# A new fixed TensorE order for an interleaved recurrent-attention and GLU kernel

## The chip, the cores and the metric

The kernel runs on one core of one Trainium2 chip. The metric is the device time of one execution in microseconds (us). The engines are named as the profile names them: PE is TensorE's matmul side, PEld its weight load, DVE is VectorE, ACT is ScalarE, POOL is GpSimd, and SP is SyncE, which here issues almost all DMAs. All of them run from their own instruction stream and meet only at semaphores.

## What is computed

A memory-augmented attention block and a gated GLU block alternate, four blocks in all, over a sequence of 2048 rows of width 448. Cut to what matters:

```
def A(x):                       # 16 heads of 256, segments of 32 rows, 8 memory rows
    mem = mem0
    for s in range(64):
        h = concat(mem, x[32*s : 32*s+32])            # 40 rows
        q, k, v = h @ Wq, h @ Wk, h @ Wv              # per head
        p = softmax(mask(q @ k.T / 16))
        o = sum over heads of (p @ v) @ Wo
        mem, out[s] = o[:8], o[8:]                    # the next segment needs this mem
def B(x):
    g = x @ W_gate
    return ((g * (g > 0)) * (x @ W_up)) @ W_down
x = x + A(layernorm(x));  x = x + B(layernorm(x))     # layer 0
x = x + A(layernorm(x));  x = x + B(layernorm(x))     # layer 1, same weights
```

The memory makes A a recurrence of 64 segments: segment s+1 cannot start its scores before `mem` of segment s is there.

## The kernel before, in words

**Set-up.** The weights of a head are folded: `M` (from Wq and Wk) gives the scores directly from h, `N` (from Wv and Wo) gives the output directly from p @ h. These products are made once, while the weights arrive by DMA.

**Steps.** After that come 68 steps (`step`, L1382). In step t, segment t of layer 0 and segment t-4 of layer 1 are worked on together, so nearly every operation handles 2 x 40 rows. Steps 0 to 3 have layer 0 alone, steps 64 to 67 layer 1 alone. A step has these PE groups, each one a run of matmuls that ends with one semaphore increment:

- `t_block` (L980): M times h; three blocks named 0, 1 and 2, each with a first part "f" on 64-row tiles and the rest "r" on the full array. ACT and DVE copy the result to `TTm` (memory rows) and `TTs` (segment rows).
- `s_mem` (L1054), the scores of the memory rows; then a softmax on DVE and ACT that ends in `Pm`; `p_t_mem` (L1127), a transpose of it on PE; a copy to `PTm`; `u_mem` (L1144), p @ h; a copy to `UTm` by ACT and DVE, half each; `un_mem` (L1158), times N; ACT copies a half to `sumA`, DVE adds the halves to `mv`, the new memory (L1176); `m_t` (L1178) transposes it for the next step. This is the recurrence.
- `s_seg` (L1076), the scores of the segment rows; a softmax on DVE and ACT that ends in `Ps`; a transposing DMA to `PTs` (`seg_pt`, L1117); four groups `u_seg0` to `u_seg3` (L1231); copies to `U` or `UTm`.
- Every second step: `un` (L1274), 28 pairs or quadruples of matmuls, U times N; a layernorm (`ln_b`, L944); a transposing DMA to `xBT`; `b_layer` (L1312), gate and up products in units of 4, 4, 4 and 2 column chunks; relu on ACT and a product on DVE to `hB`; `b_down`, seven groups. `un` and B work of one step is spread over the following steps, where it fills PE while the recurrence waits.

`m_nat` (L1201) moves the new memory with four small DMAs ("mk") and two more ("ride").

**What sets the order.** A planner inside the program (`_Order`, L320 to L510) places all 8371 operations on the engines, with a cost model of its own, before anything is emitted. Each operation has a key, and among those that could go next the smallest key wins. Keys of PE groups come from the table `SLOT` (L174), which names a group, its number and its step: `@a0` to `@a3` for the first four steps, `@z0` to `@z5` from step 64 on, and `@0` to `@3` for the step modulo 4 in between; `PERIOD` (L173) is added for every four steps. Keys of other engines' operations follow from who needs them, plus an offset from `BIAS` (L164). For steps 8 to 63 the order of the PE groups is not left to the planner: sorted by key they are chained, each a predecessor of the next (L375). So in this steady part the numbers in `SLOT` matter only by their rank, and the same order repeats every four steps. For the first and last steps they are priorities. The PSUM bank of a group, and whether a copy goes to ACT or DVE (`cp` allows both), are decided by the planner in both parts.

```
            if o.slot in SLOT:
                o.key = SLOT[o.slot] + PERIOD * (o.t // 4)
...
            o.key += sum(BIAS.get(k, 0.0) for k in bias_keys(o))
            o.prio = -o.key
        line = sorted((o for o in self.ops if o.slot in SLOT and 2 * LAG <= o.t < NSEG), key=lambda o: o.key)
        for a, b in zip(line, line[1:]):
            if a not in b.preds:
                b.preds.append(a)
```

A PE group has a mode, the tiling of the array it uses (0 whole array; 2 four column strips of 32; 3 quarters of 64 x 64). `un` and full `b_down` groups may run in mode 0 or, split into four column strips (`quarters`, L884), in mode 2; they take the mode that the array is in (L465). PSUM has eight banks, and a group that opens a new tile waits until the copies that read the bank before are done.

Of the kernel before, what the change touches and what calls it, by code (L numbers as in the profile page):

```python
# [45 lines left out]
class _Sched:  # L46
# [118 lines left out]
    "t_blockm+": 4131, "t_blocks+": 6194, "s_mem+": -350, "p_t_mem+": 7632, "u_mem+": -471, "un_mem+": -457,  # L165
    "un_memh+": -23541, "m_t+": -19808, "m_tk+": -8621, "s_seg+": -19261, "seg_pt+": -2390, "u_seg0+": -23506,
    "u_seg1+": 9252, "u_seg2+": -29593, "u_seg3+": -6650, "m_nat+": 10625, "t_block0f+": 14052, "t_block0r+": -1099,
    "t_block1r+": 22222, "t_block2r+": -17971, "ln_a+": 2217, "ln_ac+": 3345, "un+": -2521, "ln_b+": 1019,
    "b_layer+": -20861, "b_down+": -10132, "m_natx+": 7129, "stay": 2496, "win": 163,
# [5 lines left out]
    "t_block0f.0@a0": 50159, "t_block0r.0@a0": 48445, "t_block0r.1@a0": 66618, "t_block0r.2@a0": 58400,  # L175
    "t_block0r.3@a0": 37177, "t_block0r.4@a0": 67166, "t_block0r.5@a0": 95580, "t_block1f.0@a0": 81552,
    "t_block1r.0@a0": 96466, "t_block1r.1@a0": 76789, "t_block1r.2@a0": 77518, "t_block1r.3@a0": 84652,
    "t_block2r.0@a0": 4656, "s_mem.0@a0": 55973, "fills_mem.0@a0": 52862, "fills_mem.1@a0": 79245,
    "p_t_mem.0@a0": 77938, "u_mem.0@a0": -1119, "fillu_mem.0@a0": 107569, "un_mem.0@a0": 80345, "m_t.0@a0": 42261,
    "s_seg.0@a0": 71567, "u_seg0.0@a0": 100936, "u_seg1.0@a0": 91440, "u_seg2.0@a0": 80408, "u_seg3.0@a0": 56794,  # L180
    "t_block0f.0@a1": 45270, "t_block0r.0@a1": 17400, "t_block0r.1@a1": -7010, "t_block0r.2@a1": 40391,
    "t_block0r.3@a1": 82450, "t_block0r.4@a1": 52995, "t_block0r.5@a1": 62740, "t_block1f.0@a1": 63553,
    "t_block1r.0@a1": 28364, "t_block1r.1@a1": 74689, "t_block1r.2@a1": 76929, "t_block1r.3@a1": 81822,
    "t_block2r.0@a1": 67618, "s_mem.0@a1": 27449, "fills_mem.0@a1": 71144, "fills_mem.1@a1": 63924,
    "p_t_mem.0@a1": 6422, "u_mem.0@a1": 74228, "fillu_mem.0@a1": 51559, "un_mem.0@a1": 53034, "m_t.0@a1": 68700,
    "s_seg.0@a1": 67452, "u_seg0.0@a1": 69786, "u_seg1.0@a1": 83046, "u_seg2.0@a1": 92206, "u_seg3.0@a1": 76576,
    "un0.0@a1": 92765, "un0.1@a1": 79387, "un0.2@a1": 101487, "un0.3@a1": 90435, "un1.0@a1": 63322, "un1.1@a1": 69781,
    "un1.2@a1": 39275, "un1.3@a1": 40361, "un2.0@a1": 106250, "un2.1@a1": 82903, "un2.2@a1": 63137, "un2.3@a1": 42476,
    "un3.0@a1": 64407, "un3.1@a1": 71224, "b_layerf.0@a1": 139224, "b_layer.0@a1": 116387, "b_layer.1@a1": 98718,
    "b_layerf.1@a1": 143708, "b_layer.2@a1": 132409, "b_layer.3@a1": 103128, "b_down.0@a1": 127683,  # L190
    "b_down.1@a1": 126220, "b_down.2@a1": 72769, "b_down.3@a1": 112103, "b_down.4@a1": 96440, "b_down.5@a1": 113434,
    "b_down.6@a1": 125266, "t_block0f.0@a2": 37971, "t_block0r.0@a2": 12506, "t_block0r.1@a2": 60559,
    "t_block0r.2@a2": 46755, "t_block0r.3@a2": 83848, "t_block0r.4@a2": 58924, "t_block0r.5@a2": 46186,
    "t_block1f.0@a2": 28635, "t_block1r.0@a2": 60990, "t_block1r.1@a2": 72547, "t_block1r.2@a2": 53785,
    "t_block1r.3@a2": 60218, "t_block2r.0@a2": 66386, "s_mem.0@a2": 81137, "p_t_mem.0@a2": 78840, "u_mem.0@a2": 59588,
    "un_mem.0@a2": 43030, "m_t.0@a2": 39632, "s_seg.0@a2": 79148, "u_seg0.0@a2": 120824, "u_seg1.0@a2": 115627,
    "u_seg2.0@a2": 122511, "u_seg3.0@a2": 108587, "t_block0f.0@a3": 110070, "t_block0r.0@a3": 140639,
    "t_block0r.1@a3": 112726, "t_block0r.2@a3": 82684, "t_block0r.3@a3": 118188, "t_block0r.4@a3": 132793,
    "t_block0r.5@a3": 95384, "t_block1f.0@a3": 76944, "t_block1r.0@a3": 139308, "t_block1r.1@a3": 124186,
    "t_block1r.2@a3": 80065, "t_block1r.3@a3": 112387, "t_block2r.0@a3": 115734, "s_mem.0@a3": 142810,  # L200
    "p_t_mem.0@a3": 106030, "u_mem.0@a3": 151505, "un_mem.0@a3": 101197, "m_t.0@a3": 76094, "s_seg.0@a3": 97187,
    "u_seg0.0@a3": 127310, "u_seg1.0@a3": 89485, "u_seg2.0@a3": 145237, "u_seg3.0@a3": 114347, "un0.0@a3": 135091,
    "un0.1@a3": 98232, "un0.2@a3": 102557, "un0.3@a3": 118395, "un1.0@a3": 118579, "un1.1@a3": 58610,
    "un1.2@a3": 62740, "un1.3@a3": 81468, "un2.0@a3": 50475, "un2.1@a3": 78517, "un2.2@a3": 78037, "un2.3@a3": 109548,
    "un3.0@a3": 105293, "un3.1@a3": 120353, "b_layerf.0@a3": 53573, "b_layer.0@a3": 80328, "b_layer.1@a3": 92109,
    "b_layerf.1@a3": 63133, "b_layer.2@a3": 92492, "b_layer.3@a3": 34316, "b_down.0@a3": 31797, "b_down.1@a3": 101377,
    "b_down.2@a3": 71871, "b_down.3@a3": 58611, "b_down.4@a3": 86319, "b_down.5@a3": 40731, "b_down.6@a3": 55318,
    "t_block0f.0@0": 33273, "t_block0r.0@0": 36345, "t_block0r.1@0": 33785, "t_block0r.2@0": 35833,
    "t_block0r.3@0": 34297, "t_block0r.4@0": 38392, "t_block0r.5@0": 36857, "t_block1f.0@0": 29690,
    "t_block1r.0@0": 37369, "t_block1r.1@0": 30202, "t_block1r.2@0": 30714, "t_block1r.3@0": 31226,  # L210
    "t_block2r.0@0": 37880, "s_mem.0@0": 39928, "p_t_mem.0@0": 44023, "u_mem.0@0": 45559, "un_mem.0@0": 47607,
    "m_t.0@0": 50678, "s_seg.0@0": 40440, "u_seg0.0@0": 48630, "u_seg1.0@0": 49142, "u_seg2.0@0": 48119,
    "u_seg3.0@0": 51702, "t_block0f.0@1": 55285, "t_block0r.0@1": 57333, "t_block0r.1@1": 56821,
    "t_block0r.2@1": 57845, "t_block0r.3@1": 56309, "t_block0r.4@1": 58357, "t_block0r.5@1": 55797,
    "t_block1f.0@1": 52214, "t_block1r.0@1": 54261, "t_block1r.1@1": 53238, "t_block1r.2@1": 52726,
    "t_block1r.3@1": 54773, "t_block2r.0@1": 53750, "s_mem.0@1": 59380, "p_t_mem.0@1": 61940, "u_mem.0@1": 63476,
    "un_mem.0@1": 70642, "m_t.0@1": 76785, "s_seg.0@1": 59892, "u_seg0.0@1": 69619, "u_seg1.0@1": 70130,
    "u_seg2.0@1": 72178, "u_seg3.0@1": 72690, "un0.0@1": 71154, "un0.1@1": 71666, "un0.2@1": 73202, "un0.3@1": 73714,
    "un1.0@1": 74226, "un1.1@1": 74738, "un1.2@1": 75250, "un1.3@1": 75761, "un2.0@1": 76273, "un2.1@1": 77297,
    "un2.2@1": 77809, "un2.3@1": 78321, "un3.0@1": 78833, "un3.1@1": 79345, "b_layerf.0@1": 86511,  # L220
    "b_layer.0@1": 88047, "b_layer.1@1": 88559, "b_layerf.1@1": 90607, "b_layer.2@1": 87535, "b_layer.3@1": 94190,
    "b_down.0@1": 103404, "b_down.1@1": 103916, "b_down.2@1": 104428, "b_down.3@1": 104940, "b_down.4@1": 105964,
    "b_down.5@1": 108011, "b_down.6@1": 108523, "t_block0f.0@2": 82416, "t_block0r.0@2": 84464,
    "t_block0r.1@2": 82928, "t_block0r.2@2": 83952, "t_block0r.3@2": 86000, "t_block0r.4@2": 83440,
    "t_block0r.5@2": 84976, "t_block1f.0@2": 79857, "t_block1r.0@2": 80880, "t_block1r.1@2": 81904,
    "t_block1r.2@2": 80369, "t_block1r.3@2": 81392, "t_block2r.0@2": 85488, "s_mem.0@2": 87023, "p_t_mem.0@2": 89071,
    "u_mem.0@2": 90095, "un_mem.0@2": 92142, "m_t.0@2": 93678, "s_seg.0@2": 89583, "u_seg0.0@2": 101357,
    "u_seg1.0@2": 106476, "u_seg2.0@2": 101869, "u_seg3.0@2": 107500, "t_block0f.0@3": 97261, "t_block0r.0@3": 98285,
    "t_block0r.1@3": 99309, "t_block0r.2@3": 98797, "t_block0r.3@3": 100333, "t_block0r.4@3": 97773,
    "t_block0r.5@3": 99821, "t_block1f.0@3": 94702, "t_block1r.0@3": 96750, "t_block1r.1@3": 95214,  # L230
    "t_block1r.2@3": 96238, "t_block1r.3@3": 95726, "t_block2r.0@3": 100845, "s_mem.0@3": 102380,
    "p_t_mem.0@3": 105452, "u_mem.0@3": 106988, "un_mem.0@3": 109035, "m_t.0@3": 111595, "s_seg.0@3": 102892,
    "u_seg0.0@3": 109547, "u_seg1.0@3": 110571, "u_seg2.0@3": 110059, "u_seg3.0@3": 111083, "un0.0@3": 112107,
    "un0.1@3": 112619, "un0.2@3": 113130, "un0.3@3": 113642, "un0.4@3": 114154, "un0.5@3": 114666, "un0.6@3": 115178,
# [1210 lines left out]
```

## Time and profile before

| what | us |
|---|---|
| median of 7 runs | 1537.77 |
| lowest and highest of them | 1532.33, 1542.79 |
| the profiled execution's own time | 1535.18 |
| its span, first to last instruction | 1533.3 |
| PE busy in the span | 1476.5 |
| DVE busy, ACT busy | 803.2, 776.9 |
| PE in its chain of work that ended last | 82% of the span |

The profile is of one execution. "Busy" of PE counts the modelled length of each matmul, which includes its run through the array, so a busy PE can still lose time between groups; the start of one group to the start of the next is the better measure, and it is read from the timeline. The clock that the throttle granted to TensorE is listed by stretch of time; 0.50 is half speed.

### The profile page before, as it was taken

To read this page: it belongs to the slowest core of one execution; us is meant where nothing else is said; L and a number is where in the kernel's file an instruction comes from. 1 tells how busy PE (TensorE), PEld (TensorE's weight loads), DVE (VectorE), ACT (ScalarE), POOL (GpSimd) and SP (SyncE) were. 2 spreads that over 40 slices of the span, in tenths; PEclk is the share of its full clock that TensorE was granted. 3 is DMA by queue.
4 is the path that set the end of the run, shared out by engine and by line. 5 is a ranking of instruction groups with operands and counts; after the bars stand their busy time and mean duration, and the time that the engine had idled before them with its cause. 6 is when DMAs were issued, how large, how long until landed. Compare 5 with 4: busy or idle time off the path is not lost.

```text
span 1533.3 us, 88468 instructions
## 1 busy us (share of the span) xinstructions
PE 1476.5 (96%) x41051; PEld 1156.4 (75%) x41051; DVE 803.2 (52%) x2198; ACT 776.9 (51%) x2491; POOL 112.5 (7%) x259
## 2 busy tenths in 40 slices
PE   6999999999999999999999999999999999999998
PEld 2567777878787877878787787878687787878675
DVE  6545545555454555545454555545454564545554
ACT  6634444555545554555545455554555455554433
POOL 4000000000000000000000000000000000000000
PEclk9999999999999999999999999999999999999999
DMA  9751101001110111111110110011010111001010
GB/s 219 186 133 22 17 16 24 21 16 19 22 22 16 24 17 22 22 16 19 21 22 14 24 21 16 19 22 22 16 24 17 22 22 17 18 20 20 17 22 14
DMA packets 137761, 48.24 MB, mean 31 GB/s; under 512 B 125736, under 2 KB 137264, under 8 KB 137392
## 3 DMA queue, kind: packets, MB, share of 16 engines
q1 hardware_dynamic: 137040, 42.33, 14.1%
q8 instruction: 323, 5.29, 1.4%
q14 instruction: 46, 0.38, 0.1%
q10 hardware_dynamic: 352, 0.24, 0.1%
HBM read 10.33 MB, written 1.84 MB: 8 GB/s over the span
## 4 chain that ended last, share of the span: by engine, by line
PE 82%; DVE 5%; DMA 5%; SPq 4%; ACT 3%; issue 1%
PE b L139 82%; SPq L690 3%; DVE big L865 2%; DMA xBT<-xn 2%; ACT UTm L864 1%; DMA PTs<-Ps 1%; DMA xAT<-xn 1%; ACT Em L1069 1%; SPq L1211 1%; DVE UTm L865 1%; DMA ride<-mv 1%; DVE mv L1176 1%; DVE Es L1111 0%; DMA Nw<-in_A_Wo_dram 0%; ACT sumA L864 0%
## 5 line engine op out<-in xcount | busy, mean ns | idle before, releaser
L139 PE MATMUL b<-hT,Mw 128*128 128x80 bf16 (+1 forms) x11424 | 437.6, 199 | 5.1 <-issue 3.8
L139 PEld LDWEIGHTS b<-hT,Mw 128*128 128x128 bf16 x11424 | 417.6, 99 | 18.9 <-issue 7.5
L139 PE MATMUL b<-Nw,big 128*32 128x448 bf16 (+1 forms) x3840 | 294.1, 353 | 2.0 <-DMA Nw<-in_A_Wo_dram 0.6
L864 ACT ACTIVATE TTm<-b 128x80 bf16<-128x80 f32 (+5 forms) x639 | 148.8, 233 | 274.0 <-PE b L139 266.4
L864 ACT ACTIVATE TTs<-b 128x320 bf16<-128x320 f32 (+5 forms) x640 | 269.5, 421 | 5.2 <-PE b L139 4.9
L139 PE MATMUL b<-xBT,big 128*128 128x128 bf16 (+3 forms) x4900 | 207.8, 215 | 3.4 <-DMA xBT<-xn 3.2
L139 PEld LDWEIGHTS b<-Nw,big 128*32 128x32 bf16 (+1 forms) x3840 | 131.0, 97 | 105.8 <-issue 10.3
L139 PE MATMUL b<-Nw,UTm 128*32 128x224 bf16 x7504 | 197.4, 263 | 6.1 <-ACT UTm L864 5.0
L139 PEld LDWEIGHTS b<-Nw,UTm 128*32 128x32 bf16 x7504 | 178.8, 98 | 29.1 <-ACT UTm L864 13.0
L139 PEld LDWEIGHTS b<-xBT,big 128*128 128x128 bf16 (+1 forms) x4900 | 182.6, 101 | 18.0 <-DMA xBT<-xn 4.2
L865 DVE CAST TTm<-b 64x64 bf16<-64x64 f32 (+4 forms) x245 | 54.5, 223 | 198.1 <-PE b L139 194.0
L139 PE MATMUL b<-hT,M 64*64 64x80 bf16 (+3 forms) x6808 | 146.1, 199 | 3.0 <-DVE hT L865 1.5
L864 ACT ACTIVATE big<-b 128x512 bf16<-128x512 f32 (+1 forms) x228 | 111.2, 545 | 61.9 <-PE b L139 61.4
L865 DVE CAST big<-b 128x512 bf16<-128x512 f32 (+1 forms) x160 | 97.3, 624 | 65.7 <-PE b L139 65.2
L139 PEld LDWEIGHTS b<-hT,M 64*64 64x64 bf16 (+2 forms) x6808 | 110.6, 107 | 27.3 <-issue 17.2
L864 ACT ACTIVATE UTm<-b 128x512 bf16<-128x512 f32 (+2 forms) x173 | 87.1, 541 | 64.6 <-PE b L139 63.8
L865 POOL COPY hK<-xn 32x448 bf16<-32x448 bf16 x136 | 75.1, 552 | 572.8 <-DVE xn L918 563.4
L865 DVE CAST TTs<-b 64x256 bf16<-64x256 f32 (+5 forms) x244 | 102.5, 420 | 5.3 <-PE b L139 5.3
L1343 DVE TENSOR_TENSOR hB<-gT,b 128x512 bf16<-128x512 bf16 (+2 forms) x128 | 77.9, 619 | 47.6 <-ACT gT L1342 26.6
L139 PE MATMUL b<-big,hB 128*128 128x448 bf16 (+1 forms) x574 | 100.1, 353 | 0.8 <-DVE hB L1343 0.8
L1342 ACT ACTIVATE gT<-b 128x512 bf16<-128x512 f32 (+2 forms) x128 | 66.4, 538 | 63.7 <-DVE hB L1343 34.2
L864 ACT ACTIVATE sumA<-b 64x224 f32<-64x224 f32 x67 | 23.7, 353 | 135.1 <-PE b L139 135.0
(101 smaller groups left out, 1329.6 us busy)
## 6 DMA issues: line engine op xcount, KB each, us to landing
hK<-mv SPq DMA_DIRECT2D x252, 3.5 KB
big<-in_A_Wo_dram SPq DMA_DIRECT2D x3, 896.0 KB, 5.8
ride<-mv SPq DMA_DIRECT2D x124, 7.0 KB
out_dram<-ys SPq DMA_DIRECT2D x32, 56.0 KB, 2.0
big<-in_B_W_up_dram SPq DMA_DIRECT2D x7, 224.0 KB, 2.9
big<-in_B_W_gate_dram SPq DMA_DIRECT2D x7, 224.0 KB, 3.3
big<-in_B_W_down_dram SPq DMA_DIRECT2D x7, 224.0 KB, 3.2
XA<-in_A_x_dram SPq DMA_DIRECT2D x28, 56.0 KB, 2.2
```

The costliest lines, as they stand in the source:

```text
L139: ins = E.matmul(out, lhsT=lhsT, rhs=rhs, **kw)
L690: S.q.add("dma", ("sp",), {"sp": 6200.0 if w == "Wv" and q else 4100.0}, lambda E: E.dma_start_transpose(out=st[w, q], in_=src[w][:, q * 1 ...
L864: return E.activation(out(), src(), ACT.Copy, **({} if scale is None else {"scale": scale}))
L865: return E.tensor_copy(out(), src()) if scale is None else E.tensor_scalar(out(), src(), scale, None, op0=ALU.mult)
L1069: S.act(lambda E, i=i: E.activation(S.Em[:, i, :], src()[:, i, :], ACT.Exp, bias=st[:, 32 + i:33 + i], scale=1.0, accum_out=st[:, 34 + i:3 ...
L1176: S.dve(lambda E: E.tensor_tensor(S.mv[0:64, :], C.b()[0:64, 0:DH], S.sumA[:, :], ALU.add), DH, C.res(half=(0,)) + [("sumA",)], [("mem",)])
L1211: S.qdma(f"mk{l}{n}", lambda E, a=a, b=b, n=n: E.dma_start(S.hK[a:a + 8, pp, s, DH * n:DH * n + DH], S.mv[b:b + 8, :]), [("hKm", pp, s, l, ...
L1342: S.act(lambda E, g=g, R=R, n=n: E.activation(S.gT[:, g, 0:n], R[0].b()[:, 0:n], ACT.Relu), n, R[0].res(), [("gT", g)])
L1343: S.dve(lambda E, g=g, R=R, n=n, fcs=fcs: E.tensor_tensor(S.hB[:, fcs[0]:fcs[-1] + 1, 0:w], S.gT[:, g, 0:n].rearrange("p (a b) -> p a b", ...
```

## The change

One table and one list of offsets get new numbers; no operation, buffer, tile or formula changes. `BIAS` is new in every entry (`u_seg0+` is dropped). `SLOT` keeps its 480 names, of which 465 get another number. The diff, cut to its head and a few rows of the steady part:

```
 BIAS = {
-    "t_blockm+": 4131, "t_blocks+": 6194, "s_mem+": -350, "p_t_mem+": 7632, "u_mem+": -471, "un_mem+": -457,
...
-    "b_layer+": -20861, "b_down+": -10132, "m_natx+": 7129, "stay": 2496, "win": 163,
+    "t_blockm+": -901, "t_blocks+": -588, "s_mem+": -9244, "p_t_mem+": 9533, "u_mem+": -2372, "un_mem+": 5457,
...
+    "b_layer+": -14434, "b_down+": 15427, "m_natx+": 2933, "stay": 1294, "win": 173,
 }
 PERIOD = 86000.0
 SLOT = {
...
-    "t_block1r.2@2": 80369, "t_block1r.3@2": 81392, "t_block2r.0@2": 85488, "s_mem.0@2": 87023, "p_t_mem.0@2": 89071,
...
-    "p_t_mem.0@3": 105452, "u_mem.0@3": 106988, "un_mem.0@3": 109035, "m_t.0@3": 111595, "s_seg.0@3": 102892,
...
-    "b_down.6@3": 155107, "b_layer.4@1": 91630, "b_layer.5@1": 92654, "b_layer.6@1": 91119, "b_layer.7@1": 93166,
...
+    "t_block1r.3@2": 79857, "t_block2r.0@2": 83952, "s_mem.0@2": 86511, "p_t_mem.0@2": 88047, "u_mem.0@2": 89071,
...
+    "p_t_mem.0@3": 104940, "u_mem.0@3": 106988, "un_mem.0@3": 108523, "m_t.0@3": 111083, "s_seg.0@3": 101869,
...
+    "b_down.6@3": 154595, "b_layer.4@1": 90095, "b_layer.5@1": 91630, "b_layer.6@1": 92142, "b_layer.7@1": 103404,
```

What this does to the order is seen when both programs are laid side by side. In the third and the fourth step of each steady period (t mod 4 = 2 and 3) the PE groups from `s_mem` on stand like this; numbers in brackets are matmuls, and "4 x b_down" is four groups of two:

```
third step, before:  s_mem, b_layer(12), b_layer(12), b_layer(12), p_t_mem, s_seg, u_mem, b_layer-f, b_layer(6), b_layer(12), un_mem, ...
third step, after:   s_mem, b_layer(12), b_layer(12), p_t_mem, b_layer(12), u_mem, b_layer-f, b_layer(12), s_seg, un_mem, ...

fourth step, before: u_seg0, u_seg2, s_mem, s_seg, 4 x b_down, p_t_mem, b_down, u_seg1, u_mem, u_seg3, 2 x b_down, un_mem,
                     u_seg0, u_seg2, u_seg1, u_seg3, m_t, un ...
fourth step, after:  u_seg2, u_seg0, s_mem, s_seg, 2 x b_down, b_layer(6), 2 x b_down, p_t_mem, b_down, u_seg1, u_seg3, u_mem, 2 x b_down, un_mem,
                     u_seg0, u_seg3, u_seg1, u_seg2, m_t, un ...
```

(The `u_seg` groups ahead of `u_mem` are those of the third step, the last four those of the fourth.) The first and second step change less: groups of `un` move by some places among the `t_block` groups, and in the second step `p_t_mem` stands after two `b_layer` groups, not three. Over the whole program the matmul count goes from 41051 to 41135, since one `un` group in each steady period now falls into mode 2 (eight quarter matmuls for two). Changes of mode go from 803 to 801: 45 in each steady period in both, six fewer in steps 2 and 3, two more in steps 4 to 7 and two more from step 64 on. 25 copies move from DVE to ACT. On SP the same 607 DMAs are issued; in the steady part the four "mk" DMAs now stand ahead of the two "ride" DMAs at every step; before, they did so at one step of four (t mod 4 = 1), and behind them at the other three.

## The prediction

> **What bounds the kernel now.** I read the page first, then busy time by stage, the timeline of one steady period, and the windows in which the clock fell.
>
> ```profile
> span 1533.3 us, 88468 instructions
> ...
> PE 1476.5 (96%) x41051; PEld 1156.4 (75%) x41051; DVE 803.2 (52%) x2198; ACT 776.9 (51%) x2491; POOL 112.5 (7%) x259
> ```
>
> PE bounds it; DVE and ACT are half idle. Stages (stretch, its length, then each engine's busy time and count, clock, DMA), cut at the start of step 0, of step 4, of the steady part (8, 60) and of step 64:
>
> ```profile
> 0.00:63.44 63.44, 47.74 (x361) 22.26 (x362) 38.58 (x122) 42.02 (x122) 18.44 (x31) 0.97 1.07 237
> 63.44:132.56 69.12, 63.91 (x1857) 46.78 (x1856) 30.59 (x110) 28.21 (x96) 3.43 (x10) 1.00 0.36 87
> 132.56:217.51 84.95, 76.33 (x2424) 62.73 (x2420) 44.55 (x120) 41.47 (x137) 5.85 (x14) 0.96 0.11 19
> 217.51:1352.36 1134.85, 1116.73 (x31510) 891.30 (x31506) 599.70 (x1587) 589.52 (x1884) 75.72 (x182) 1.00 0.11 20
> 1352.36:1450.10 97.74, 97.19 (x2736) 76.44 (x2737) 49.19 (x133) 47.72 (x157) 5.93 (x15) 1.00 0.09 17
> 1450.10:1533.30 83.20, 74.64 (x2178) 56.92 (x2175) 40.57 (x128) 27.97 (x97) 3.11 (x8) 0.98 0.10 18
> ```
>
> The 13 periods of the fourth row average 87.3 us, of which PE is busy 85.9. So reordering can only touch little there. What is left is seen from starts of groups on PE, at the end of the period with steps 28 to 31:
>
> ```profile
> 728.14 1.67 PE L139 MATMUL b<-big,hB 128*128 128x448 bf16 x8
> 729.92 0.23 PE L139 MATMUL b<-ident,Pm 128*128 128x128 bf16 x1
> ...
> 731.11 0.93 PE L139 MATMUL b<-big,hB 128*128 128x448 bf16 x4
> 732.28 2.87 PE L139 MATMUL b<-Nw,UTm 128*32 128x224 bf16 x112 [0.24 <-ACT UTm L864]
> 735.08 1.25 PE L139 MATMUL b<-PTs,hK 40*64 40x512 bf16 x16
> 736.25 0.27 PE L139 MATMUL b<-selm,mv 128*32 128x16 bf16 x16
> 736.62 2.83 PE L139 MATMUL b<-Nw,big 128*32 128x448 bf16 x56
> ```
>
> A 448-column matmul starts every 0.189 us, so eight from 728.14 would let `p_t_mem` start at 729.65: it waits **0.27**. Four from 731.11 and a change of mode (0.09, the start-to-start of `un` to `t_block-f` is 0.283 against 0.189) lead to 731.96; `un_mem` waits **0.31**, for ACT. Within the row at 735.08 the fourth `u_seg` waits **0.27** for the bank that `mv`'s addition frees, and `un` at 736.62 waits **0.25** for a copy. With 0.04 at `s_seg` that is 1.15 us per period, the same in every period I compared. Beyond it come waits for late DMAs (`xBT`, `PTs`; 6.5 us over ten places from step 35 on) and stalls inside groups without a wait (0.05 to 2.6 us per period), which no order of groups addresses.
>
> **The change, part by part.**
>
> *Instructions.* 84 more matmuls, all from `un` pairs that run as eight quarters. A pair takes 0.378 us; the 56 quarters at 736.62 are seven groups spaced 0.378: no cost. Mode changes: 45 per period in both; their kinds differ slightly, +0.04 per period.
>
> *Fourth step, `p_t_mem`.* `b_layer`(6) now stands before it, six matmuls at 0.056 = 0.335 more cover against a wait of 0.27: **-0.27**. This holds even if DVE is again held up by `u_seg0` copies ahead of the softmax, as before (`Pm` done 2.77 us after `s_mem`'s start; PE now arrives after 0.21 + 0.81 + 4 x 0.378 + 0.335 = 2.87). What is late next is `u_mem`, whose chain (transpose, 0.28 copy) has `b_down`, `u_seg1` and now also `u_seg3` as cover: no wait.
>
> *Third step, `p_t_mem`.* It loses one `b_layer`(12), 0.67 us, of its cover. The row before:
>
> ```profile
> 708.33 0.37 PE L139 MATMUL b<-hT,TTm 128*128 128x40 bf16 x8
> 708.55 2.17 PE L139 MATMUL b<-xBT,big 128*128 128x128 bf16 x36
> 710.55 0.22 PE L139 MATMUL b<-ident,Pm 128*128 128x128 bf16 x1
> ```
>
> `Pm` is ready 1.82 us after `s_mem`'s start in this step (DVE unhindered) and a semaphore takes 0.055 to PE: 1.87. PE arrives after 0.21 + 2 x 0.67 = 1.55. A new wait of **+0.32**. Behind it on PE stand `b_layer`(12) and everything else; nobody can pass.
>
> *Fourth step, `un_mem`.* Before, ACT had copies of `u_seg1` (0.60) and `u_seg3` (0.38) ahead of its half of `u_mem`'s copy, and finished 1.53 us after `u_mem`'s start. Now `u_seg3` goes to DVE and both halves follow one copy: they end 1.18 after `u_mem`'s start (DVE, last), against two `b_down` and a mode change of 0.32 + 0.38 + 0.47 = 1.17; with the semaphore a wait of 0.07: **-0.24**. If the copies queued as before it would be the old chain with 0.22 less cover: +0.2. The order of copies is fixed and DVE is free there, so I take the first.
>
> *Bank and `un`.* The fourth `u_seg` becomes a 512-column one behind the short one: its predecessors give 0.08 less cover, **+0.08**; `un` then waits less for its copy, **-0.10**. `s_seg`'s 0.04 goes.
>
> Sum per period: -0.27 + 0.32 - 0.24 + 0.08 - 0.10 - 0.04 + 0.04 = -0.21; x 14 periods = **-2.9 us**.
>
> *DMA order.* "Ride" moves behind four "mk" issues, 4 x 0.67 us later, at three steps. The step whose `ride` precedes `xBT` closely (t mod 4 = 1) had this order already; elsewhere `ride` has some 9 us before `un_mem` may overwrite its source. "Mk" comes earlier. Cost nothing. The fourth step's `PTs` transpose is issued 0.34 us sooner and its user comes 0.18 sooner, so the waits of 0.86, 0.89, 0.46 and 0.47 (steps 47 to 59) shrink by 0.16 each: **-0.6**. `xBT` keeps its distance. The third step's `s_seg` moves behind three groups; its `PTs` then lands 1 us later, with 9 us to spare.
>
> *First and last steps.* With the same group durations and chains I get: steps 2 and 3 six mode changes fewer (-0.6), bank and `mv` waits +0.5, steps 4 to 7 two more changes (+0.4), waits -0.8; at the seam in step 8 waits of 0.24 (`m_t`) and 0.40 (`t_block1f`) go, less the 0.25 counted above (-0.4); step 64 on: waits -0.9, changes and spacing +0.7; small moves in step 0 and the set-up 0.1. Sum about **-1.1 us**, which I bound by -3 and +2.
>
> *The clock.* Here row and rule differ. The five stretches below are clock windows of 3.41 us:
>
> ```profile
> 161.33:164.74 3.41, 1.55 (x57) 1.18 (x57) 2.54 (x9) 1.56 (x6) 0.00 (x0) 1.00 0.02 5
> 164.74:168.15 3.41, 3.41 (x80) 3.04 (x76) 0.70 (x3) 0.00 (x0) 0.00 (x0) 0.50 0.21 43
> ...
> 205.70:209.11 3.41, 1.36 (x49) 1.09 (x53) 2.46 (x7) 1.99 (x6) 0.00 (x0) 1.00 0.04 9
> 209.11:212.52 3.41, 3.41 (x84) 3.13 (x76) 0.00 (x0) 0.00 (x0) 0.00 (x0) 0.50 0.19 39
> 89.65:93.06 3.41, 1.89 (x80) 1.64 (x71) 0.38 (x1) 0.35 (x1) 0.00 (x0) 1.00 0.94 180
> ```
>
> With PE busy 1.55 and 1.36 us of a window the next ran at 0.50 and lost 1.7 us; at 1.89 it did not. The Trainium skill ("TensorE: Matmul & The Clock Gate", section "Why this matters for your kernels") asks for no idle gap above about 3 us between bursts. By that rule no gap of steps 4 to 7, none above 1.3 us, could cost clock, and the change gains or loses nothing by it. By the row the sum of short waits counts. Step 7's three waits before `un_mem` (1.2 + 0.9 + 0.8) become 0.3 + 0.9 + 1.2, which still can fall into one window; step 5 is unchanged; step 4 gains a wait (`u_mem` 0.44), leaving PE busy near 1.9. I take 0, with -1.7 and +1.7 as ends.
>
> Sum: -2.9 - 0.6 - 1.1 = -4.6 us. The profiled execution (1535.18, span 1533.3) stands 2.6 below the median 1537.77; the difference is applied to the median: **1533 us**.
>
> **Rivals.** *Nothing to be told from noise:* medians of this kernel can be told apart from about 0.3% on (4.6 us; its runs spread over 10), and my sum lies at that edge. If the third step's new wait is paid and `un_mem` keeps 0.31, a period changes by +0.03 and only about -1.5 remains: 1536. For it: both rest on copies queued differently on ACT and DVE, planned, not measured.
>
> *Slower, by late DMAs:* `PTs` in the fourth step must land 3.6 us after its issue; it took 2.42 in nine periods and 3.96 to 4.40 in four. Why is not visible, so the new order of DMAs can shift which periods are hit. The ten waits are six for `xBT` (0.63 on average) and four for `PTs` (0.67, now less 0.16). If all 14 periods had both, PE would pay 16 instead of 6.5 us: +9.5, with -2.9 and -1.1 from the rest, gives 1543; with the longest of each seen (1.31 and 0.73) it would be 1556. It decides once these waits sum to 15 us. Against: the "mk" and "ride" packets are far from the `PTs` issue in time, and the order ahead of `xBT` is as before.
>
> *It does not do what it says:* excluded for the order itself, since the two programs' orders differ as listed.
>
> **How the numbers follow.** Faster by over 0.3%, ending 1526 to 1533: 0.55 (the sum holds, or the first steps or the clock add to it). Within 0.3%: 0.30. Slower: 0.15. The range takes the bounds of first steps, clock and part of the DMA case: 1526 to 1543; the likeliest case's own range is 1526 to 1533.
>
> **What would show it.** Right: in steady periods `p_t_mem` of the fourth step starts with no wait, that of the third waits 0.32 for DVE's `Pm`, `un_mem` of the fourth waits under 0.1, and a period without late DMA takes 86.1 us where it took 86.3. Wrong: `PTs` or `xBT` waits in most periods, a half-speed window inside the steady part, or stalls inside groups that grow.

## The result, and the profile after

| | before | after |
|---|---|---|
| median (runs) | 1537.86 (31) | 1531.53 (12) |
| lowest, highest | 1532.33, 1543.15 | 1525.96, 1533.78 |
| ratio of the times, 95% interval | | 0.9950 [0.9937, 0.9964] |
| profiled execution, its span | 1535.18, 1533.3 | 1526.03, 1524.2 |

Two more runs of programs with the changed order (below) gave 0.9969 and 0.9952, so the gain is 5 to 8 us. I had forecast 1533.0, which is 4.8 us less than 1537.8. The number held; most of the terms that make it up did not.

The page of after, its span and busy line:

```profile
span 1524.2 us, 88674 instructions
...
PE 1474.7 (97%) x41135; PEld 1156.4 (76%) x41135; DVE 793.4 (52%) x2173; ACT 784.8 (51%) x2516; POOL 113.0 (7%) x259
```

PE is as busy as before (1476.5), so the time came out of its gaps. The stages of after, cut at the same events as before (steps 4 to 7, 8 to 59, 60 to 63, 64 to the end):

```profile
132.00:215.49 83.49, 75.16 (x2432) 61.27 (x2428) 42.51 (x114) 42.84 (x143) 5.82 (x14) 0.98 0.11 19
215.49:1344.40 1128.91, 1117.49 (x31586) 893.18 (x31583) 590.88 (x1561) 597.37 (x1910) 76.27 (x182) 1.00 0.11 20
1344.40:1441.54 97.14, 96.70 (x2738) 76.34 (x2735) 48.54 (x130) 48.10 (x159) 5.88 (x14) 1.00 0.09 17
1441.54:1524.20 82.66, 73.41 (x2178) 55.84 (x2175) 41.08 (x131) 27.27 (x94) 3.05 (x8) 1.00 0.09 18
```

Steps 8 to 59 take 1128.9 us where they took 1134.9, a period 86.8 where it took 87.3. The fourth step of the period with steps 28 to 31, in the timeline of PE of after:

```profile
725.26 0.92 PE L139 MATMUL b<-big,hB 128*128 128x448 bf16 x4
726.02 0.50 PE L139 MATMUL b<-xBT,big 128*128 128x128 bf16 x6
726.35 0.92 PE L139 MATMUL b<-big,hB 128*128 128x448 bf16 x4
727.11 0.22 PE L139 MATMUL b<-ident,Pm 128*128 128x128 bf16 x1
...
728.28 0.93 PE L139 MATMUL b<-big,hB 128*128 128x448 bf16 x4
729.28 2.87 PE L139 MATMUL b<-Nw,UTm 128*32 128x224 bf16 x112
732.07 0.73 PE L139 MATMUL b<-PTs,hK 40*64 40x512 bf16 x12
733.02 0.41 PE L139 MATMUL b<-PTs,hK 40*64 40x512 bf16 x4 [0.21 <-DVE mv L1178]
```

`p_t_mem` at 727.11 follows `b_down` at once: four matmuls at 0.189 from 726.35. Its wait of 0.27 is gone. From 728.28, 4 x 0.189 and 0.095 for the change of mode lead to 729.13; `un_mem` starts at 729.28 and still waits 0.13 to 0.15, where 0.31 stood. The fourth `u_seg` at 733.02 waits 0.38 from start to start where it waited 0.27. The third step of the same period:

```profile
706.27 0.37 PE L139 MATMUL b<-hT,TTm 128*128 128x40 bf16 x8
706.49 1.50 PE L139 MATMUL b<-xBT,big 128*128 128x128 bf16 x24
708.15 0.23 PE L139 MATMUL b<-ident,Pm 128*128 128x128 bf16 x1 [0.16 <-DVE Pm L1075]
```

Two `b_layer`(12) end their slots at 706.49 + 24 x 0.056 = 707.83, and `p_t_mem` comes at 708.15: the new wait of 0.32, in all 14 periods. (The 0.16 in the row is idle time after the modelled end of the matmuls ahead.)

To compare whole steady parts, I took the start-to-start times of all groups from each trace and subtracted what the same group needs where nothing is late. Another choice of that baseline moves the last two columns by about 1 us. "Late DMA" is the sum of waits for `xBT` and `PTs` in the 14 periods of steps 8 to 63; "stalls" is lost time inside groups, where no semaphore is waited for. "Program" is the label of an experiment below. The programs ran on several chips, on which the kernel before had medians from 1533.5 to 1538.4, and each ratio is to the kernel before on the same chip: rows are compared by their ratios, not by their medians. None of the profiles has a half-speed window in steps 8 to 63.

| program | median | ratio to before [95%] | steps 8 to 63 | late DMA | stalls |
|---|---|---|---|---|---|
| before, first profile | 1537.86 | | 1232.6 | 6.5 | 8.2 |
| copy_before | 1536.65 | 1.0002 [0.9987, 1.0018] | 1230.6 | 5.8 | 7.8 |
| shift_before | 1535.61 | 0.9993 [0.9980, 1.0006] | 1230.3 | 6.3 | 6.9 |
| after, first profile | 1531.53 | 0.9950 [0.9937, 0.9964] | 1226.1 | 3.3 | 6.3 |
| copy_after | 1533.08 | 0.9969 [0.9954, 0.9983] | 1224.6 | 2.9 | 5.2 |
| shift_after | 1526.26 | 0.9952 [0.9935, 0.9969] | 1223.6 | 4.3 | 3.4 |
| ends_only | 1531.65 | 0.9973 [0.9957, 0.9989] | 1228.4 | 4.1 | 9.9 |
| steady_only | 1536.58 | 1.0017 [1.0003, 1.0031] | 1223.6 | 3.2 | 4.3 |
| third_back | 1526.92 | 0.9934 [0.9912, 0.9957] | 1222.9 | 7.8 | 6.1 |
| lock_good | 1525.31 | 0.9921 [0.9901, 0.9940] | 1220.5 | 3.4 | 4.8 |
| lock_bad | 1532.49 | 0.9956 [0.9939, 0.9974] | 1228.7 | 8.2 | 8.8 |
| before_lock | 1533.30 | 0.9977 [0.9961, 0.9992] | 1230.3 | 1.3 | 10.4 |

The three profiles with the order of before average 1231.2 us in steps 8 to 63, the three with the order of after 1224.8: 6.4 us less. That is about the whole gain: the three ratios give 6.6 us on average.

### The profile page after: what moved, and what is told of

It reads as the page before. It is cut to its first block, busy times and chain, and to the rows that moved or that the text cites. A ratio compares the mean times of both kernels' runs of the same rounds, so it can differ in the third digit from the quotient of the medians.

```text
span 1524.2 us, 88674 instructions
## 1 busy us (share of the span) xinstructions
PE 1474.7 (97%) x41135; PEld 1156.4 (76%) x41135; DVE 793.4 (52%) x2173; ACT 784.8 (51%) x2516; POOL 113.0 (7%) x259
## 4 chain that ended last, share of the span: by engine, by line
PE 81%; DVE 8%; DMA 5%; SPq 3%; ACT 2%; issue 1%
PE b L139 81%; SPq L692 3%; DMA PTs<-Ps 2%; DVE UTm L867 1%; DMA xBT<-xn 1%; ACT Em L1071 1%; DVE big L867 1%; DMA xAT<-xn 1%; DVE stat L1115 1%; DVE Ps L1117 1%; DVE stat L1112 0%; ACT Es L1114 0%; DVE mv L1178 0%; DVE stat L1069 0%; DVE Es L1113 0%
## 5 line engine op out<-in xcount | busy, mean ns | idle before, releaser
L139 PE MATMUL b<-Nw,big 128*32 128x448 bf16 (+1 forms) x3924 | 298.8, 353 | 0.8 <-DMA Nw<-in_A_Wo_dram 0.8
L866 ACT ACTIVATE TTs<-b 128x320 bf16<-128x320 f32 (+5 forms) x666 | 281.6, 423 | 3.6 <-PE b L139 3.5
L866 ACT ACTIVATE TTm<-b 128x80 bf16<-128x80 f32 (+5 forms) x667 | 156.3, 234 | 245.4 <-PE b L139 239.3
L139 PE MATMUL b<-xBT,big 128*128 128x128 bf16 (+3 forms) x4900 | 211.8, 215 | 1.4 <-DMA xBT<-xn 1.0
L139 PE MATMUL b<-Nw,UTm 128*32 128x224 bf16 x7504 | 194.0, 261 | 3.8 <-ACT UTm L866 1.6
L867 DVE CAST TTm<-b 64x64 bf16<-64x64 f32 (+5 forms) x217 | 47.5, 219 | 198.8 <-PE b L139 196.0
L1344 ACT ACTIVATE gT<-b 128x512 bf16<-128x512 f32 (+1 forms) x128 | 66.9, 543 | 86.2 <-PE b L139 50.3
L866 ACT ACTIVATE UTm<-b 128x512 bf16<-128x512 f32 (+2 forms) x159 | 83.6, 555 | 51.1 <-PE b L139 49.1
L867 DVE CAST TTs<-b 64x256 bf16<-64x256 f32 (+4 forms) x218 | 88.4, 406 | 3.0 <-PE b L139 3.0
L139 PE MATMUL b<-PTs,hK 40*64 40x512 bf16 (+1 forms) x1024 | 77.4, 361 | 6.0 <-DVE mv L1178 2.7
```

The source lines that it names most:

```text
L139: ins = E.matmul(out, lhsT=lhsT, rhs=rhs, **kw)
L866: return E.activation(out(), src(), ACT.Copy, **({} if scale is None else {"scale": scale}))
L867: return E.tensor_copy(out(), src()) if scale is None else E.tensor_scalar(out(), src(), scale, None, op0=ALU.mult)
L1344: S.act(lambda E, g=g, R=R, n=n: E.activation(S.gT[:, g, 0:n], R[0].b()[:, 0:n], ACT.Relu), n, R[0].res(), [("gT", g)])
```

## The theory to be tested

My account of the result: part of the gain is the order of groups, as forecast; the larger part is fewer late DMAs and fewer stalls, which the forecast did not have. The second part needs a cause. In the trace the instructions of PE come in packets of 16 KB: 323 packets in the profile of before, whose program has 82675 PE instructions (a weight load and a matmul each time, and the semaphore waits), so 256 to a packet, one about every 4.6 us. A transposing DMA (`PTs`, `xBT`, `xAT`) lands 2.41 us after its issue, or 3 to 4.4. In the first profiles of before and after, all 118 of those over 2.6 us in steps 8 to 63 had an instruction packet under way. One of them in before, step 47, from the rows for 1082 to 1087 us (queue 8 carries the packets of PE's instructions):

```profile
q8 instruction: 1, 0.02, 1.1%
...
PTs<-Ps SPq DMA_TRANSPOSE x1, 4.4
```

Theory: where the boundary of a packet falls in a period decides which transposes are late and where PE runs out of instructions. Rival: both wander by chance, or follow the kernel's other DMAs.

A period of before has 4882 PE instructions, 19 packets and 18 instructions, so the boundary moves by 18 per period, through 252 of 256 places in 14 periods. One of after has 4895 and moves by 31.

## Experiments on late DMAs and stalls

**copy_before**, no edit.

> The kernel before, unchanged. It asks whether the steps in which the transposing DMAs land late belong to the program or to the execution. Theory (each 16 KB packet of instructions collides with the transpose that is under way, and the packets are placed by the instruction stream): the late ones fall at the same steps as in the profile of before, PTs of the fourth step at 47, 51, 55 and 59 and xBT of the fourth step from 35 to 59; the waits for PTs and xBT in the steady part sum to 6.5 us again, within 1; ratio 1.000. Rival (chance of each execution): late at other steps, the sum anywhere from 2 to 15 us.

The late `PTs` came at steps 43 to 55, one period sooner than in the first profile, the wait for DMAs was 5.8 us, the ratio 1.0002. The pattern belongs to the program; its edges move a little between executions.

**shift_before**

```diff
-        S.mm(lambda: [MM(T.b().bitcast(BF)[:, c * 8:c * 8 + 8], S.mNc[...
+        S.mm(lambda: [MM(T.b()[:, 256:288], S.ident[:, :], S.ident[:, 0:32], start=True, stop=True) for _ in range(64)] +
+             [MM(T.b().bitcast(BF)[:, c * 8:c * 8 + 8], S.mNc[...
```

> The kernel before with 64 matmuls of 32 columns more in the set-up, whose result nobody reads: 128 instructions of PE, half a 16 KB packet at 64 bytes each; the order of groups is that of before. Theory of the packets: the waits between groups stay (p_t_mem 0.27, un_mem 0.31, fourth u_seg 0.27, un 0.25 in the fourth step), the late PTs and xBT move to other steps, the waits for them change from 6.5 us to some other sum by 2 us or more; 64 short matmuls cost 0 to 3 us in the set-up. Rival (lateness is set by what else the kernel moves by DMA, or by chance): the same steps are late as before, sum 6.5 within 1; or a pattern without order.

The waits at the groups stayed (sums over 14 periods: 3.71 for `p_t_mem`, 4.37 for `un_mem`). The late `PTs` of the fourth step moved to steps 11 to 31, by 28 to 36 steps: seven to nine periods of 18 instructions, 126 to 162, for the 128 put in. For some of the 14 `PTs` of each trace, the start of the instruction packet, counted from the issue of the `PTs`, then its landing, also from the issue, us:

```
before        step 39: 2.28, 2.42   47: 2.32, 4.37   51: 2.39, 4.40   55: 1.91, 3.96   59: 1.88, 3.98   63: -0.04, 2.41
shift_before  step 11: 1.86, 3.95   23: 1.99, 4.01   31: 1.95, 4.15   35: -0.05, 2.87  47: 3.17, 2.44   59: 2.34, 2.42
after         step 27: 2.33, 2.42   31: 2.34, 2.42   35: 2.34, 4.35   39: 1.82, 3.94   43: -0.21, 2.56  51: 3.06, 2.43
```

A packet that starts 1.8 to 2.2 us after the issue, before this transpose is done, makes it 1.5 to 1.8 us late; from 2.2 to 2.4 it can go either way (and costs 2.0 if it goes wrong); in these rows one that starts at the issue costs under 0.5, and one after the landing nothing. Between these places the cost rises: over all transposes of the twelve profiles with one packet in that time, the median landing was 2.9 us after the issue for packets that started near 0.4, 3.7 near 1.0 and 4.0 near 2.0. But the sum of the waits did not move (6.3), against what I had written: a run goes through a whole cycle of places wherever it starts, and meets the bad ones once.

Over all twelve profiles of the table, 701 of the 706 late transposes of steps 8 to 63 had an instruction packet under way in the 2.4 us after their issue, and some 360 of the 638 on time. So nearly every late one has a packet in that time, but the packet alone does not make it late: its place decides.

**Stalls.** They show as a group that is cut in two. Step 31 of before, two neighbouring rows of the PE timeline:

```profile
721.73 0.46 PE L139 MATMUL b<-hT,Mw 128*128 128x80 bf16 x8
722.64 3.21 PE L139 MATMUL b<-hT,Mw 128*128 128x80 bf16 x85 [0.46 <-issue]
```

Inside one `t_block` nothing is waited for, yet PE stands still ("issue"). I numbered the PE instructions from the program. Of 133 gaps over 0.23 us inside groups (0.32 for 448 columns and more) in steps 8 to 63 of the twelve profiles, 131 end at number 193 or 194 of 256. The packet begun last started 2.2 to 2.9 us before PE went on. I read this as PE waiting for it; no row of a trace names the packet as what ended the wait. Most lie in `t_block` groups, whose matmuls of 80 columns start every 0.011 us (64 x 64 tiles) to 0.036 us (whole array), so that packets are asked for every 4 us.

**lock_good** and **lock_bad**. Both start from third_back (below), and both put two `un` groups behind the next step's first group, where they run in mode 0, two matmuls each:

```diff
-    "un0.1@3": 112107, ... "un0.6@3": 114666, "un0.7@3": 115178,
+    "un0.1@3": 112107, ... "un0.6@3": 116000, "un0.7@3": 116100,
+        ... for _ in range(32)]     # lock_good, set-up; 102 in lock_bad
```

> The changed kernel with its third step undone, and two un pairs of step 4k+3 moved behind the first group of the next step, where they run as two matmuls each and not as eight quarters: a period of four steps then has 4869 PE instructions and not 4893, 19 packets of 256 and 5 over and not 29. 32 unread short matmuls in the set-up (64 instructions) start the periods at instruction 80 of a packet; the last begins at 140. Theory (both the late transposes and the stalls inside groups are set by where the packet boundary falls in a period; in the traces so far, starts from 80 to 135 are the shortest periods): every period takes 86.0 to 86.5 us where the same order without the lock took 85.9 to 87.3; steps 8 to 63 lose 5 to 8 us against it, about 1519 to 1522 in all, ratio to before 0.989 to 0.991. Rival (the place of the boundary is a bystander; waits wander by chance): 1527, ratio 0.993 to 0.994, and periods that still differ by over 1 us.

> The same order of groups as the kernel with the good start, but 102 unread short matmuls in the set-up instead of 32, so that the periods start from instruction 220 to 280 (24) of a packet. Theory of the packet boundary: late PTs, late xBT or stalls inside t_block groups in nearly every period, 86.8 to 87.5 us each, 10 to 17 us more than with the good start, ratio to before 0.996 to 1.001. Rival (bystander): the same time as with the good start, to within the 70 short matmuls (0 to 2 us).

Steps 8 to 63 of both, lock_good first:

```profile
220.44:1440.97 1220.53, 1211.20 (x34161) 968.96 (x34162) 633.88 (x1677) 646.02 (x2083) 81.66 (x196) 1.00 0.11 20
218.00:1446.69 1228.69, 1212.54 (x34161) 969.25 (x34161) 633.48 (x1677) 647.36 (x2083) 82.29 (x196) 1.00 0.10 20
```

Medians 1525.3 and 1532.5 on the same chip, so the place of the boundary is no bystander: same order of groups, 7.2 us apart (8.2 in steps 8 to 63). Late DMA 3.4 against 8.2 us, stalls 4.8 against 8.8. Both effects are smaller than I wrote. With the good start a period took 85.8 to 86.8, mean 86.3, not always under 86.5: stalls of 0.5 to 0.8 us came in four of the 14 periods, at places that I had taken for free of them. Against third_back the lock gained 2.3 us in steps 8 to 63, not 5 to 8, and the medians' intervals overlap.

**before_lock**

```diff
-    ... "un0.6@3": 115178,
+    ... "un0.6@3": 117700,
+        ... for _ in range(116)]    # set-up
```

> The kernel before, with one un pair more behind the first groups of the next step (two matmuls and not eight quarters): 4870 PE instructions in a period and not 4882, 6 over 19 packets and not 18; 116 unread short matmuls in the set-up set the start of the periods to 90, the last to 162. No other part of the change is in it. Theory: periods of 86.3 to 86.9, mean 86.5, instead of 86.3 to 88.8, mean 87.3: 8 to 12 us faster than before, ratio 0.992 to 0.995, though the waits of the order (0.27 before p_t_mem, 0.31 before un_mem) all stay; that is more than the change itself brings. Rival (bystander): ratio 1.000.

A miss. Late DMA fell to 1.3 us, as the theory has it, but stalls rose to 10.4, from 1.0 to 2.5 us per period once the boundary stood at 138 to 162. In before and shift_before such places had cost 0.2 to 1.1. Steps 8 to 63 took 1230.3, as before; the median is 0.2% lower, of which I can show no part. So the place tells where a stall falls, but not how long it is; what else sets the length stays open.

**shift_after**: the 64 short matmuls in the changed kernel.

> The changed kernel with the same 64 unread short matmuls in the set-up as were put into the kernel before: its 14 steady periods then start half a packet of instructions later. It asks whether the changed order itself waits less for late DMAs (3.3 and 2.9 us in its two profiles, where the order of before waited 5.8 to 6.5), or whether that hung on the packet boundaries it met. Order: the sum for PTs and xBT stays at 3 to 4 us. Boundaries: it moves by 2 us or more, to 5 us or above or near 1. The waits of 0.32, 0.13, 0.38 and 0.15 at the groups stay in both cases. Time: ratio to before 0.994 to 0.998, which tells nothing apart.

4.3 us: by the mark that I had set, nearer the answer "order" than "boundaries". With the order of after, four profiles (steady_only has its steady order too) waited 2.9 to 4.3 us for late DMAs, three with that of before 5.8 to 6.5. But ends_only has the steady PE order of before too and waited 4.1, before_lock, one group of it moved, 1.3, and third_back, close to the order of after, 7.8. So the order alone does not set this sum. In the first profiles the order of after met late `PTs` of the fourth step in two periods, that of before in four. Its boundary moves by 31 and not by 18 per period, and so is out of the bad places sooner; but it also goes round 1.7 times and not once. Whether the step of 31 or the place of the groups saves the waits was not tried and stays open.

## Experiments on the order of groups

**ends_only**: the `BIAS` of after, its slots `@a..` and `@z..`, and the slots `@0` to `@3` of before.

> The change without the new steady order: the new offsets of the groups and the new slots of first and last steps, the slots of the steady steps as before. Theory (DVE takes the softmax of the fourth step ahead of u_seg0's copies because of the new offsets alone): the wait of 0.27 before the fourth step's p_t_mem goes though b_layer(6) does not stand before it, the third step's p_t_mem does not wait, un_mem keeps 0.30; a steady period gains 0.26 and the ends 1 us, together about 4.5 us against before, ratio 0.997. Rival (what my forecast said, the cover of b_layer(6) removes it): the wait of 0.27 stays, and only the 1 us of the ends comes, ratio 0.999. Either may be off by 3 us through the late DMAs.

The theory held and a step of my forecast fell. `p_t_mem` of the fourth step does not wait here though no `b_layer`(6) stands ahead of it; the timeline of PE:

```profile
729.13 1.67 PE L139 MATMUL b<-big,hB 128*128 128x448 bf16 x8
730.64 0.22 PE L139 MATMUL b<-ident,Pm 128*128 128x128 bf16 x1
```

Eight at 0.189 from 729.13 are 730.64. The reason stands on DVE, first in before, then in ends_only:

```profile
727.00 0.69 DVE L865 CAST UTm<-b 128x512 bf16<-128x512 f32 x1 [1.50 <-PE b L139]
727.60 0.68 DVE L865 CAST big<-b 128x512 bf16<-128x512 f32 x1
728.20 0.23 DVE L1067 TENSOR_REDUCE stat<-b 128x2 f32<-128x80 f32 x1
```

```profile
727.98 0.69 DVE L867 CAST UTm<-b 128x512 bf16<-128x512 f32 x1 [0.72 <-PE b L139]
728.59 0.23 DVE L1069 TENSOR_REDUCE stat<-b 128x2 f32<-128x80 f32 x1
728.74 0.68 DVE L867 CAST big<-b 128x512 bf16<-128x512 f32 x1
```

The first step of the softmax, the small reduction, used to stand behind two copies of `u_seg` and now stands behind one: 0.60 us sooner on the recurrence, for a wait of 0.27. No new slot of the steady steps is needed for that; in after DVE takes the same order. Whether `b_layer`(6) would have been enough by itself was not tried. `un_mem` keeps its wait (4.38 us over 14 periods), and the steady part is 2.8 us below the three profiles of before.

**third_back**, the changed kernel with the third step undone:

```diff
-    "b_layer.1@1": 88559, ...   "s_seg.0@2": 90607, ...
+    "b_layer.1@1": 87800, ...   "s_seg.0@2": 88300, ...
```

> The changed kernel with one part undone: in the third step one b_layer(12) stands before p_t_mem again and s_seg before u_mem. Theory (the moved b_layer(12) took 0.67 us of cover from a softmax that needs 0.32 of it): the wait of 0.32 in front of the third step's p_t_mem goes in all 14 periods and nothing comes in its place, 4 to 4.5 us faster than the changed kernel, so about 10 to 11 us faster than before, ratio 0.993. Rival (the cover is only moved: b_layer(12) is now missing before un_mem or s_seg's results come too early for the banks): the time is that of the changed kernel, ratio 0.995 to 0.996. Late DMAs may move either by 3 us.

The timeline of its third step:

```profile
708.63 0.37 PE L139 MATMUL b<-hT,TTm 128*128 128x40 bf16 x8
708.84 2.17 PE L139 MATMUL b<-xBT,big 128*128 128x128 bf16 x36
710.85 0.22 PE L139 MATMUL b<-ident,Pm 128*128 128x128 bf16 x1
```

708.84 + 36 x 0.056 = 710.86: no wait, in none of 14 periods (4.5 us in after), and nothing came in its place at `un_mem`. The median is 0.66% below before, as the theory said. Against the three profiles of after, steps 8 to 63 gained only 1.9 us, because this program met 7.8 us of late DMA, 4.3 more than they did on average. lock_good has the same order and 3.4.

**copy_after**, no edit.

> The changed kernel again, on the chip of the others. Theory: the new steady order costs 0.32 per period at the third step's p_t_mem, so this is 3 to 6 us slower than the same without it (0.993 to 0.994 of before), ratio 0.995; stalls of over 0.15 us inside groups of short matmuls fall in the same steps as in its first profile (13, 17, 21, 25, 45, 49, 51, 57), the late PTs of the fourth step at 35 and 39.

Ratio 0.9969, against 0.9934 for third_back on another chip: 5 us, within the 3 to 6 that I had written for the new wait of the third step. lock_good on the same chip had 0.9921, but there the boundary is locked as well. The stalls fell in steps 13, 17, 21, 25 and 45 again, not in 49, 51 and 57; the `PTs` of steps 35 and 39 were late again (4.25 and 3.15 us).

**steady_only**: the `BIAS` of after, its slots `@0` to `@3`, and the slots `@a..` and `@z..` of before.

> The counterpart of the run with the new ends: new offsets and the new slots of the steady steps, the slots of the first and last steps as before. It prices the new slots of the ends by their absence. Theory (what the profiles so far say: without their half-speed windows, the parts outside steps 8 to 63 take 294 us with either set of ends): the same time as the changed kernel, 1531 to 1534, ratio 0.995 to 0.997; the steady part (steps 8 to 63) takes 1224 to 1227 us. Rival (my forecast's term): the ends bring 1.1 us, so 1533 to 1534, or up to 3 us: 1535, ratio 0.998. The planner's own times put it 6 us behind the changed kernel, which would be ratio 0.999.

My theory fell. The steady part took 1223.6 us as expected, but the rest of the span 313.4, against 297.8 to 305.7 in the three profiles of after: steps 4 to 7 took 88.8 us and step 64 to the last PE instruction 87.9, where the first profile of before has 85.0 and 79.5. The offsets are added to the keys of the first and last steps as well, and slots made for the old offsets no longer fit; the planner's own 6 us, which I had written down as the outsider, was close. A good part of the loss is clock: this profile has nine half-speed windows, where those of after have two to seven, and its twelve runs were granted 0.9912 on average, those of after 0.9945. A window of 3.41 us at half speed lowers the mean of a run by 0.0011, so that is about three windows more in a run, an estimate of 5 us. With nine windows at 1.7 us taken out, 298 of the 313.4 us remain. The new slots of the ends are thus needed to hold the place, not a gain: with half-speed windows taken out at 1.7 us each, the parts outside steps 8 to 63 take 293.9 us on average with the order of before (three profiles) and 293.7 with that of after (three).

## Why the prediction was right, and where it was not

- **`p_t_mem`, fourth step, -0.27 per period**: right (3.72 us over 14 periods to none). The cause given, the cover of `b_layer`(6), was not needed: ends_only has none of it. The case it was worked for, DVE held up again by the copies, did not come: DVE's order changed.
- **`p_t_mem`, third step, +0.32**: right, 0.324 in each period; third_back shows that it can be had back.
- **`un_mem`, -0.24**: the mechanism held (it needs the new steady order; ends_only keeps 0.31), the size was -0.18: 0.13 remains, not 0.07.
- **Bank wait +0.08, `un` -0.10, `s_seg` -0.04, modes +0.04**: the first two measured +0.11 and -0.11 in periods without a late `PTs`; the last two I did not measure again. The sum per period is then -0.27 + 0.32 - 0.18 + 0.11 - 0.11 - 0.04 + 0.04 = -0.13, and **-1.8 us** over 14 periods where I had -2.9. The shortest single periods are 86.06 (the first of after) and 86.28: the forecast said 86.1 and 86.3. That is 0.22 apart and not 0.13. Adding up the median length of every group over the periods gives 86.25 to 86.33 in the three profiles of before and 86.09 to 86.19 in those of after, 0.15 apart, so I keep the smaller figure and count the fit of the single periods as chance.
- **Late DMAs, -0.6**: the term that was mis-sized most. Waits of every kind in steps 8 to 63 fell by 4.6 us, average of three profiles against three; less the 1.8 above, 2.8 are due to late DMAs and what they hide.
- **Stalls, taken as something that no order addresses**: this step failed. They fell by 2.7 us (7.6 to 5.0, averages of three). lock_good and lock_bad show that stalls hang on the number of PE instructions ahead of a group (4.8 against 8.8 us), and the order changes that number through the form of one `un` per period. That this is what made them fall between before and after is argued, not shown.
- **Ends, -1.1** (its parts as written add to -1.0): not seen; -0.2 with the clock taken out. The bounds of -3 and +2 hold it.
- **Clock, 0**: right on average. Half-speed windows numbered four, three and six in the profiles of the order of before, three, seven and two in those of after (first profile, copy, shift). The clocks of the single runs are on record too: 0.9937 on average for copy_after and 0.9938 for before beside it, but 0.9960 for shift_after and 0.9932 for before beside it, so that part of the gain of this last pair is clock.

In all -1.8 - 2.8 - 2.7 - 0.2, and 0.6 lost between groups without a wait (2.3 to 2.9 us), is -6.9 us, against 6.6 from the three ratios (0.5%, 0.31%, 0.48% of 1538). So the forecast of -4.6 was close with terms of -2.9, -0.6 and -1.1 that came out as -1.8, -5.5 with the stalls, and -0.2. The direction of the order term was reasoned; that the total came so near was luck, since most of the gain came from terms that the forecast had at -0.6 and at nothing. The rival "noise-level" lost through late DMAs and stalls: the order alone would have given 1536, the figure it named, though by another sum (it had `un_mem` keep its 0.31). The rival "slower by late DMAs" named one of the mechanisms, with the wrong sign.

On the clock the prediction weighed the Trainium skill ("TensorE: Matmul & The Clock Gate", section "Why this matters for your kernels", no idle gap above about 3 us) against the windows of before. After agrees with the row, not with a rule of single gaps; two stretches of one window each in step 7, by busy time:

```profile
202.66:206.07 3.41, 1.37 (x37) 0.57 (x33) 3.30 (x10) 2.44 (x6) 0.00 (x0) 1.00 0.02 5
206.07:209.48 3.41, 3.41 (x80) 3.04 (x81) 1.92 (x5) 0.50 (x2) 0.91 (x2) 0.50 0.19 38
```

PE was busy 1.37 of 3.41 us with no single wait over 1.3, and by the rule of single gaps no clock would have been lost. The next window ran at half speed, for a loss of 1.7 us. But the sum alone does not decide either: from 76.36 of after PE was busy 2.21 us of a window and the next ran at 0.50 too.

## What to carry over

When the order of a stream of many short instructions changes, count the instructions of a period as well as their times: here the place of the boundary between packets of 256 instructions, held nearly still over the periods, moved the time by 7 us with the order of groups unchanged. Read a wait on the recurrence from the queue of the engine that releases it, since a small reduction taken ahead of a copy there was worth the same as cover on the waiting engine. And test a part of a searched table by undoing it: of this change one edit per period was a loss of 4.5 us of waits, and of the versions without it lock_good (0.9921, with the boundary locked as well) beats both kernels.

## What the runs showed of the hardware

- A transposing DMA took 2.41 us from issue to landing, and mostly 3.9 to 4.4 when a 16 KB instruction packet of PE started 1.8 to 2.2 us after the issue (shift_before, and the twelve profiles together). A packet itself took 0.88 to 1.8 us.
- Where short matmuls follow each other (80 columns, 0.036 us apart on the whole array), PE stood still for up to 1.05 us with nothing to wait for (shift_before, step 61), and 131 of 133 such gaps came at the same place of a packet of 256 instructions. That it had run out of instructions is my reading.
- A change of the array's tiling between two groups cost 0.09 us from start to start (0.283 against 0.189).
- The same program had three and seven half-speed windows in two profiles of after, at up to 1.7 us each. Over the twelve runs of after the time falls as the granted clock rises (0.992 to 0.997, correlation -0.74); 0.005 is between four and five windows, about 7.7 us by the same estimate, as much as the spread of these runs.
